# Six cumulative-sum matrices made on the chip by selects instead of loaded, fewer fillers, and a new written order of steps

## The chip, the cores and the metric

The kernel runs on one core of a Trainium2 chip, in one launch. A core has five engines that work from queues of their own: TensorE (PE, matrix products), VectorE (DVE), ScalarE (ACT), GpSimd (POOL), and SyncE (SP), which here mostly starts transfers. They meet through semaphores. Data lies in SBUF (128 partitions); PE writes its products into eight banks of PSUM. The metric is the time of one execution in microseconds on the device: the median of the runs, and lower is better.

## The reference, cut to what matters

Three stages follow one another. An SSM scan over 768 positions for 4 sequences and 8 heads gives 3072 tokens of 256 numbers; an MLP with a squared ReLU follows; then a mixture of experts in which each token goes to one of eight experts.

```python
log_a = np.log(np.clip(a, 1e-06, 1.0))
for c in range(nc):                              # 24 chunks of 32 positions
    cum = np.cumsum(la, axis=-1)                 # within the chunk
    L = np.exp(cum[:, :, :, None] - cum[:, :, None, :]) * causal
    M = np.einsum('bhin,bhjn->bhij', Cc, Bc) * L
    y_intra = np.einsum('bhij,bhjd->bhid', M, xc)
    y_inter = np.einsum('bhin,bhnd->bhid', Cc, state) * np.exp(cum)[:, :, :, None]
    state = decay_full[:, :, None, None] * state + np.sum(Bx, axis=2)
...
h = x @ w_in                                     # (3072, 256) x (256, 2048)
x = (np.maximum(h, 0.0) ** 2) @ w_out            # (3072, 2048) x (2048, 256)
...
logits = xn @ en.T / tau                         # 8 experts
e = np.argmax(logits, axis=1)
out = gate_w * (np.maximum(x @ w1[e], 0.0) @ w2[e])
```

## The kernel before, in words

Tokens are worked in 24 tiles of 128, and the tiles in 6 groups of 4. The scan does a whole tile (128 positions, four chunks of 32) with products on PE: scores of C and B (L821), a multiply by decays on VectorE (L839), a causal select on GpSimd (L847), the product with x (L932), the carried state (L883 and L891, and L899 on GpSimd, which needs `bm_s`, made from c2 in L854) and its product (L927). The decays are exponentials of cumulative sums of log a; PE makes them by multiplying log a with six constant 128x128 matrices, `wm_s[:, 0]` to `wm_s[:, 5]`. Matrices 0 to 3 serve `tables` (L1066), matrix 5 `tables2` (L1080), matrix 4 `tables2` too (L1082) and `ssm_ct0` (L768), which scales C of tiles 0 to 3. Before, the six come with two loads of the constant c1 into the tile `c1_s`: one of 128 x 263 (matrices 4 and 5 and seven columns more), one of 128 x 512 (matrices 0 to 3). A second constant, c2, holds other tables.

In the MLP a unit is 128 of the 2048 hidden columns for one group of 512 tokens, 16 units to a group. Each operand is a pair of 16-bit parts. For a unit, PE does the first product into bank 0 or 1 (L1266), ScalarE the ReLU (L1290), ScalarE or VectorE the square (L1295, L1298), ScalarE the upper part (L1302), VectorE or GpSimd the subtraction that gives the lower part (L1306, L1309), and PE the second product into banks 2 and 3 (L1285). The units of group 0 have code of their own (L1175 and L1214; L1247 and L1250 are their subtractions). `DUE["s2"]` and `DUE["v2"]` are the shares of the units of groups 2 to 5 whose squares are done by ScalarE, and whose subtractions by VectorE. Where a group is done, tokens are routed: logits (L1379), the expert and its weight (L1423 to L1434 on VectorE), places in the expert's list (L1439 to L1445 on PE). For groups 4 and 5 these products lie in bank 7, which shares one tile of PSUM with bank 6, so an instruction on one of the two banks may have to wait for the other. The experts then work in 28 jobs of 128 tokens: first product (L1651, two banks of 0, 1, 4, 5), ReLU and lower part (L1752, L1754), second product (L1692 with L1702, in bank 6 or 2), result (L1719).

All work is written as threads (Python generators) that yield a step at a time with its engine. `weave(th, ORDER)` issues the steps in the order of the list ORDER, one number for each step: it is the thread whose next step is issued. So ORDER alone sets the order of each engine's queue, SP's and GpSimd's among them; what waits for what on the chip follows from the data. A model of the engines' times runs along (`free`, `late`, the numbers that the steps yield); what it decides is how many fillers stand ahead of a step of PE. A filler is a matmul on zeros, 128 x 176, whose result nothing reads (`keep_warm`, L484); 26 stand at the very start. Loads go out on SP (L492), each yielding its step and then `Q.dma_start`. There are eight semaphores for such transfers, used in turn, so the ninth waits for the first to land, and so on. `wide` weights (w_in, w_out) come in four parts each and are converted (L549, L559, L586, L649 to L656) before they are used.

Line numbers here are those of the kernel before. In the changed kernel the same lines stand a little further on: L484 is L485, L492 is L493, L1379 is L1380, and from there to the threads' list five are added, as L1423, now L1428 (L839, L847, L871, L899, L927 and L1066 keep theirs).

## Time and profile before

| | us |
|---|---|
| median of 3 runs (496.10 to 496.74) | 496.70 |
| the profiled execution | 497.33 |
| its span (first to last event of the trace) | 495.6 |
| PE busy | 481.8 (97%) |
| DVE, ACT, POOL busy | 326.9, 345.1, 171.7 |
| DMA moved | 64.52 MB, mean 130 GB/s |

Times in the rows are in us from the span's start unless marked ns. A row of a timeline is one instruction, or several of one kind (x6 is their number), with the time for which the engine had been idle before it and whose end released it. `bank<-wexp` is a product of data in the tile `wexp` into a bank. Matmuls are pipelined: the starts of two that follow one another tell their rate better than their durations. A filler counts as busy. The granted clock is the share of full speed that the throttle granted.

### The profile page before, as it was taken

Reading aid. Unit: us, or ns where it says so; the run is one execution under the profiler, and the core shown is the slowest. Engines: PE = TensorE matmul, PEld = TensorE weight load, DVE = VectorE, ACT = ScalarE, POOL = GpSimd, SP = SyncE. Lnnn points to the kernel's source line nnn. Section 1 sums busy time; section 2 is a strip of 40 time slices with the busy share of each in tenths; the row PEclk is TensorE's granted clock in tenths of the full one; section 3 lists DMA queues with packets and bytes.
Section 4 is the critical chain, followed back from the end, with each engine's and each line's share of the span. In section 5 each row is a group of like instructions: output and inputs, shape, how many; then the busy total and the mean of one; then the engine's idle time right before and its main releaser. Section 6 shows DMA issues by size and latency. Waiting matters only on the chain.

```text
span 495.6 us, 11923 instructions
## 1 busy us (share of the span) xinstructions
PE 481.8 (97%) x4116; PEld 316.1 (64%) x4116; DVE 326.9 (66%) x918; ACT 345.1 (70%) x715; POOL 171.7 (35%) x194
## 2 busy tenths in 40 slices
PE   8999999999999999999999999999899999999994
PEld 8775567677666776767667666766455555555553
DVE  4799988578997889967566865875673343233331
ACT  4799995698879989999999999976332243232321
POOL 2487798544584234600300030030013220220332
PEclk9999999999999999999999999999999999999999
DMA  8970014337155381517224324017887989985980
GB/s 285 400 291 2 2 54 113 102 85 204 16 178 154 44 241 27 151 38 243 72 92 134 113 102 118 13 55 111 140 166 182 196 142 158 188 146 96 158 161 33
DMA packets 112363, 64.52 MB, mean 130 GB/s; under 512 B 101277, under 2 KB 105775, under 8 KB 109232
## 3 DMA queue, kind: packets, MB, share of 16 engines
q1 hardware_dynamic: 105632, 57.22, 47.1%
q0 software_dynamic: 2496, 6.40, 4.4%
q10 hardware_dynamic: 4176, 0.13, 0.8%
q8 instruction: 36, 0.59, 0.5%
q14 instruction: 23, 0.19, 0.1%
HBM read 32.52 MB, written 8.13 MB: 82 GB/s over the span
## 4 chain that ended last, share of the span: by engine, by line
PE 82%; DMA 7%; issue 4%; POOL 3%; DVE 2%; SPq 1%; POOLq 0%; ACT 0%; ACTq 0%; DVEq 0%
PE bank L1266 23%; PE bank L1285 21%; PE bank L1651 12%; PE bank L1692 6%; DMA out<-work 4%; PE bank L1702 3%; PE bank L1214 2%; PE bank L932 2%; PE bank L821 2%; DMA wexp<-in_bc 2%; PE bank L1175 2%; PE bank L927 1%; PE bank L1000 1%; POOL wexp L847 1%; PE bank L1379 1%
## 5 line engine op out<-in xcount | busy, mean ns | idle before, releaser
L1266 PE MATMUL bank<-work 128*128 128x256 f16 x1152 | 135.9, 273 | 1.4 <-POOL work L1250 1.4
L1266 PEld LDWEIGHTS <-work 128*128 128x128 f16 x1152 | 111.9, 98 | 22.8 <-POOL work L1250 1.9
L1285 PE MATMUL bank<-work 128*128 128x512 f16 x480 | 113.3, 379 | 0.0
L1651 PE MATMUL bank<-wexp,work 128*128 x336 | 77.2, 379 | 1.6 <-DVE work L1754 1.6
L1285 PEld LDWEIGHTS <-work 128*128 128x128 f16 x480 | 46.4, 99 | 43.9 <-issue 0.2
L1692 PE MATMUL bank<-wexp,work 128*128 x216 | 71.4, 379 | 0.0
L1754 DVE SCALAR_TENSOR_TENSOR work<-bank,work 128x512 f16<-128x512 f32 x56 | 37.5, 686 | 48.6 <-ACT work L1752 48.6
L1477 POOL DMA_INDIRECT xs<-work x24 | 29.0, 1208 | 105.8 <-ACT work L1302 70.9
L1752 ACT ACTIVATE work<-bank 128x512 f16<-128x512 f32 x56 | 32.2, 597 | 43.6 <-PE bank L1651 36.1
L1726 POOL DMA_INDIRECT out<-work x28 | 27.5, 981 | 97.8 <-DVE work L1719 80.5
L1702 PE MATMUL bank<-wexp,work 128*128 x224 | 60.7, 273 | 0.0
L1306 DVE TENSOR_TENSOR work<-work 128x512 f16<-128x512 f32 x68 | 48.3, 717 | 17.5 <-ACT work L1302 17.3
L1651 PEld LDWEIGHTS <-work 128*128 128x128 f16 x336 | 32.5, 98 | 37.4 <-issue 1.7
L847 POOL TENSOR_SCALAR_AFFINE_SELECT wexp<-wexp 128x512 f32<-128x512 f32 x48 | 37.5, 781 | 53.0 <-DVE wexp L839 30.5
L1290 ACT ACTIVATE work<-bank 128x512 f32<-128x512 f32 x80 | 46.4, 588 | 9.2 <-PE bank L1285 5.6
L1302 ACT CAST work<-work 128x512 f16<-128x512 f32 x80 | 48.4, 613 | 3.4 <-PE bank L1266 2.9
L1709 ACT ACTIVATE work<-bank,work 128x256 f32<-128x256 f32 x28 | 13.2, 474 | 50.4 <-PE bank L1702 43.1
L839 DVE TENSOR_TENSOR wexp<-bank,wexp 128x256 f32<-128x256 f32 x96 | 38.2, 415 | 3.2 <-PE bank L1379 0.8
L1295 ACT ACTIVATE work<-work 128x512 f32<-128x512 f32 x64 | 39.6, 627 | 0.5
L1692 PEld LDWEIGHTS <-work 128*128 128x128 f16 x216 | 21.1, 98 | 25.4
L1719 DVE SCALAR_TENSOR_TENSOR work<-bank,work 128x256 f32<-128x256 f32 x28 | 13.4, 481 | 31.7 <-ACT work L1709 30.0
L1702 PEld LDWEIGHTS <-work 128*128 128x128 f16 x224 | 21.9, 98 | 4.8
(249 smaller groups left out, 755.9 us busy)
## 6 DMA issues: line engine op xcount, KB each, us to landing
wexp<-in_w SPq DMA_DIRECT2D x8, 1024.0 KB, 7.0
work<-in_w SPq DMA_DIRECT2D x8, 1024.0 KB, 4.9
wexp<-in_w_in SPq DMA_DIRECT2D x4, 1024.0 KB, 8.7
wexp<-in_w_out SPq DMA_DIRECT2D x4, 1024.0 KB, 13.7
wexp<-in_x SPq DMA_DIRECT2D x6, 512.0 KB, 6.2
wexp<-in_ct SPq DMA_DIRECT2D x6, 256.0 KB, 7.4
wexp<-in_bc SPq DMA_DIRECT2D x6, 256.0 KB, 5.9
xs<-work SPq DMA_DIRECT2D x9, 132.0 KB, 2.5
```

Of the source, the lines that this page charges most:

```text
L839: V.tensor_tensor(mv, ps.rearrange("p (a b) -> p a b", b=32), eg[:, t, n * q:n * q + n].rearrange("p h q -> p (h q)").unsqueeze(2) .to_bro ...
L847: G.affine_select(out=mm, in_=mm, pattern=[[0, 4], [1, P]], compare_op=ALU.is_ge, fill=0.0, base=0, channel_multiplier=-1)
L1266: T.matmul(po, gg[:, s], wout[:, wi, f], start=(f == 0 and n == 0 and k % 2 == 0), stop=(f == NF - 1 and n == 2), skip_group_check=True)
L1285: T.matmul(p, win[:, wi, kk, f * P:(f + 1) * P], x[:, xi * 2 + kk], start=(n == 0), stop=(n == 5))
L1290: S.activation(r, p, AF.Relu, scale=XK)
L1295: S.activation(r, r, AF.Square)
L1302: S.copy(gh, r)
L1306: V.tensor_tensor(gl, r, gh, ALU.subtract)
L1651: T.matmul(p, xj[i][:, xi * 2 + kk], W[:, bass.ds(e, 1), c0:c0 + 512].rearrange("p a b -> p (a b)"), start=(n == 0), stop=(n == 5))
L1692: T.matmul(po, r[:, f], w2(f, 0, 2 * DM), start=(f == 0), stop=False, skip_group_check=True)
L1702: T.matmul(bank[pbank(j)][:, 0:DM], rT[j % 4][:, 8 + f], W[:, bass.ds(es[j], 1), c0:c0 + 256].rearrange("p a b -> p (a b)"), start=False, ...
L1754: V.scalar_tensor_tensor(out=rh[:, 1, s], in0=p, scalar=0.0, in1=rh[:, 0, s], op0=ALU.max, op1=ALU.subtract)
```

## The change

The two loads of the matrices go, and a new thread `shapes` makes them in `c1_s`: three memsets on VectorE, then nine `affine_select` on GpSimd (a select keeps elements where a linear function of partition and column is at least 0, and writes a constant elsewhere). Only the seven columns behind the matrices (3.5 KB) and the small `rr` are still loaded from c1. `ssm_ct0` waits for matrix 4 and not for c1 and C before its product; it needs C only for its last multiply. The fillers at the start are 22 instead of 26 (21 and one that the model adds), and those behind them 52 instead of 72. `s2` goes from 0.875 to 0.7, `v2` from 1 to 0.92. For groups 4 and 5 the model now knows that routing holds banks 6 and 7 (`mbs`). ORDER is new throughout; of its 2272 numbers before and 2275 now the diff shows a line each.

```diff
-           a2=0.043, ..., s0=1636976993, s1=0.5, s2=0.875, bs=1, qx=84.622, qb=89.036, qc=19.985, q0=89.631,
+           a2=0.043, ..., s0=1636976993, s1=0.5, s2=0.7, bs=1, qx=84.622, qb=89.036, qc=19.985, q0=89.631,
-           pd=95.005, oe=83.994, lj=-6.608, l0=199.952, v0=0.75, v1=0.25, v2=1, ps=176, wq=-6.586, c0=71.046,
+           pd=95.005, oe=83.994, lj=-6.608, l0=199.952, v0=0.75, v1=0.25, v2=0.92, ps=176, wq=-6.586, c0=71.046,
 ORDER = (
-    "0 379 1 5.1 3 5.0 2 9 5.2 10 5.3 4 11 25 12 6.0 16 6.1 379 17 17 7 18 380 47 26 22 23 23 7 7 47 19 7 379 380 "
+    "0 5.0 5.1 1 9 25 5.2 25.0 2 5.3 10 4 11 6.0 12 3 379 3 3 3 17 17 7 380 18 47 21 7 7 379 7 379 26 19 380 47 "
...
     def load_group(g):
...
-        if g == 0:
-            yield "order", ("c1", 0)
         if g:
-            yield "spawn", load(bg[i], bc_tok[:, 4 * g:4 * g + 4, 0], 0.8, ("bc", g), late=1.5 * (g < 2))
+            yield "spawn", load(bg[i], bc_tok[:, 4 * g:4 * g + 4, 0], 0.8, ("bc", g), late=(1.0, 1.5, 0.0)[min(g, 2)])
         else:
-            yield "spawn", load(flat(beo[i][:, 0]), b_t, 0.75, ("bt", g))
+            yield "spawn", load(flat(beo[i][:, 0]), b_t, 0.75, ("bt", g), late=0.8)
...
     def ssm_ct0(k0, k1):
...
-        for key in ("la", "c1", "ct"):
-            yield "need", (key, 0)
+        yield "need", ("la", 0)
...
         V.tensor_copy(lr.rearrange("p (a n) -> p a n", n=N), lf.unsqueeze(2).to_broadcast([P, n * H, N]))
+        yield "need", ("w4", 0)
         yield "T", 0.25 * n, (0,)
...
         S.activation(et, p, AF.Exp)
+        yield "need", ("ct", 0)
         yield "V", 0.07 + 0.135 * n, "L"
...
     def tables2(i):
...
-        yield "need", ("c1", 0)
+        yield "need", ("w4", 0)
+        yield "need", ("w5", 0)
...
-        yield "T", 0.15, (mbk(g),)
+        yield "T", 0.15, mbs(g)
...
+    def mbs(g):
+
+        return (4,) if g < 4 else (6, 7)
...
-        yield "V", VS, (mbk(g),)
+        yield "V", VS, mbs(g)
         V.tensor_tensor(lg, pl, bc8(tq), ALU.mult)
...
+    def shapes():
+
+        w4, w5, w03 = c1_s[:, 4 * P:5 * P], c1_s[:, 5 * P:6 * P], c1_s[:, 0:4 * P]
+        b4 = w4.rearrange("p (a b) -> p a b", b=32)
+        q03 = w03.rearrange("p (q j) -> p q j", j=P)
+        own = c1_s[:, 0:4 * (P + 32)].rearrange("p (q r) -> p q r", r=P + 32)[:, :, 0:32]
+
+        def keep(x, pattern, base, k, fill):
+            G.affine_select(out=x, in_=x, pattern=pattern, compare_op=ALU.is_ge, fill=fill, base=base,
+                            channel_multiplier=k)
+
+        yield "V", 0.5
+        V.memset(w4, -0.5)
+        V.memset(w5, 1.0)
+        V.memset(w03, 1.0)
+        yield "G", 0.75
+        keep(w4, [[-1, P]], -1, 1, 0.5)
+        keep(b4, [[-32, 4], [0, 32]], 0, 1, 0.0)
+        keep(b4, [[32, 4], [0, 32]], 31, -1, 0.0)
+        yield "mark", ("w4", 0)
+        yield "G", 0.25
+        keep(w5, [[-1, P]], -1, 1, 0.0)
+        yield "mark", ("w5", 0)
+        yield "G", 2.3
+        keep(q03, [[32, 4], [0, P]], -1, -1, 0.5)
+        keep(q03, [[32, 4], [0, P]], 31, -1, 0.0)
+        keep(q03, [[0, 4], [-1, P]], -1, 1, 0.0)
+        keep(own, [[-32, 4], [-1, 32]], -1, 1, -0.5)
+        keep(own, [[-32, 4], [0, 32]], 0, 1, 0.0)
+        yield "mark", ("c1", 1)
...
-    k0 = 4 * P, 6 * P + 7
-    th = [(-1e3, log_inputs()), (DUE["lc"], load(c1_s[:, k0[0]:k0[1]], c1[:, k0[0]:k0[1]], 0.5, ("c1", 0))),
-          (DUE["lc"], load(rr_s, c1[0:H, k0[1]:], 0.05, ("c1", 2))), (DUE["lc"], load(c1_s[:, 0:k0[0]], c1[:, 0:k0[0]], 0.75, ("c1", 1), late=1.0)),
-          (DUE["qc"], load(c2_s, c2, 0.75, ("c2", 0), late=1.4)), (2, load_group(0)), (DUE["l1"], load_group(1)), (DUE["ct0"], ssm_ct0(0, 1)), (DUE["ct0"], halves())]
+    k0 = 6 * P + 7
+    th = [(-1e3, log_inputs()), (DUE["lc"], load(c1_s[:, 6 * P:k0], c1[:, 6 * P:k0], 0.1, ("c1", 0))),
+          (DUE["lc"], load(rr_s, c1[0:H, k0:], 0.05, ("c1", 2))), (DUE["lc"], shapes()),
+          (DUE["qc"], load(c2_s, c2, 0.75, ("c2", 0), late=1.0)), (2, load_group(0)), (DUE["l1"], load_group(1)), (DUE["ct0"], ssm_ct0(0, 1)), (DUE["ct0"], halves())]
...
-        keep_warm(26)
-        free.update(T=5.0, S=1.8, V=1.0, G=0.6, Q=0.8)
+        keep_warm(21)
+        free.update(T=4.3, S=1.8, V=1.0, G=0.6, Q=0.8)
         weave(th, ORDER)
```

How the queues stand, at two places. First SP's first transfers; `in_bc` is B by tokens, the load that the state's products need, and `in_b_t` and `in_ct` are B and C as the scores need them. Before:

```order
L492 DMA wexp_71<-in_c1 128x263
L492 DMA wexp_71<-in_ct 128x512
L492 DMA wexp_71<-in_c1 128x512
L492 DMA wexp_71<-in_b_t 128x512
L492 DMA wexp_71<-in_c1 8x128
L492 DMA wexp_71<-in_w_in 128x2048
L492 DMA wexp_71<-in_x 128x1024
L492 DMA wexp_71<-in_w_in 128x2048
L492 DMA wexp_71<-in_bc 128x4x128
L492 DMA wexp_71<-in_c2 128x512
```

and now:

```order
L493 DMA wexp_71<-in_b_t 128x512
L493 DMA wexp_71<-in_ct 128x512
L493 DMA wexp_71<-in_c1 128x7
L493 DMA wexp_71<-in_w_in 128x2048
L493 DMA work_72<-in_emb 8x256
L493 DMA wexp_71<-in_x 128x1024
L493 DMA work_72<-in_tau 128x1
L493 DMA wexp_71<-in_c1 8x128
L493 DMA wexp_71<-in_bc 128x4x128
L493 DMA wexp_71<-in_w_in 128x2048
L493 DMA wexp_71<-in_c2 128x512
```

The two large loads of c1 are gone and b_t is first; B now has one part of w_in ahead of it instead of two; the second stands between B and c2.

The first instructions of GpSimd, before:

```order
L1790 IOTA work 128x18
L1791 IOTA work 128x24
L1805 IOTA work 128x1
L847 AFFINE_SELECT wexp<-wexp 128x512
L751 TENSOR_TENSOR wexp<-wexp 128x512
L847 AFFINE_SELECT wexp<-wexp 128x512 x2
L871 TENSOR_TENSOR wexp<-wexp 128x128
L854 TENSOR_TENSOR wexp<-wexp 128x128
L847 AFFINE_SELECT wexp<-wexp 128x512
L899 TENSOR_TENSOR wexp<-wexp 128x128
```

and now:

```order
L1796 IOTA work 128x24
L1891 AFFINE_SELECT wexp<-wexp 128x128 x4
L1891 AFFINE_SELECT wexp<-wexp 128x512 x3
L1891 AFFINE_SELECT wexp<-wexp 128x4x32 x2
L847 AFFINE_SELECT wexp<-wexp 128x512 x2
L871 TENSOR_TENSOR wexp<-wexp 128x128
L847 AFFINE_SELECT wexp<-wexp 128x512
L750 TENSOR_TENSOR wexp<-wexp 128x512
L847 AFFINE_SELECT wexp<-wexp 128x512
L854 TENSOR_TENSOR wexp<-wexp 128x128
L899 TENSOR_TENSOR wexp<-wexp 128x128
L847 AFFINE_SELECT wexp<-wexp 128x512
```

The nine selects of `shapes` (L1891) stand behind the two IOTAs and ahead of everything that the scan asks of GpSimd; the IOTA of L1805 has gone further back.

The second place is the change from the last routing to the jobs. VectorE before, where bank6 is the tile of banks 6 and 7 and L1754 the lower part of a job's hidden columns, which frees bank 0, 1, 4 or 5:

```order
L1423 TENSOR_TENSOR work_72<-bank6_69,work_72 128x32
L1425 TENSOR_REDUCE work_72<-work_72 128x4
L1427 TENSOR_TENSOR work_72<-work_72 128x32
L1430 SCALAR_TENSOR_TENSOR work_72<-work_72 128x32
L1754 SCALAR_TENSOR_TENSOR work_72<-bank0_63,work_72 128x512
L1432 TENSOR_REDUCE work_72<-work_72 128x4
L1434 TENSOR_TENSOR work_72<-work_72 128x32
L1754 SCALAR_TENSOR_TENSOR work_72<-bank4_67,work_72 128x512
L1754 SCALAR_TENSOR_TENSOR work_72<-bank1_64,work_72 128x512
```

and now:

```order
L1428 TENSOR_TENSOR work_72<-bank6_69,work_72 128x32
L1430 TENSOR_REDUCE work_72<-work_72 128x4
L1432 TENSOR_TENSOR work_72<-work_72 128x32
L1435 SCALAR_TENSOR_TENSOR work_72<-work_72 128x32
L1437 TENSOR_REDUCE work_72<-work_72 128x4
L1439 TENSOR_TENSOR work_72<-work_72 128x32
L1454 TENSOR_TENSOR work_72<-bank6_69,work_72 128x32
L1724 SCALAR_TENSOR_TENSOR work_72<-bank6_69,work_72 128x256
L1759 SCALAR_TENSOR_TENSOR work_72<-bank0_63,work_72 128x512
L1456 TENSOR_TENSOR work_72<-work_72,bank6_69 128x8
L1759 SCALAR_TENSOR_TENSOR work_72<-bank1_64,work_72 128x512
```

L1754 of bank 0 stood behind four instructions of the routing; L1759, the same, now stands behind six of them, L1454 and the result of a job, L1724. PE at the same place, before, from the end of a job's second product:

```order
L1692 MATMUL bank_69<-wexp,work 128x512
L1702 LDWEIGHTS work
L1702 ISA
L1702 MATMUL bank_69<-wexp,work 128x256
L1651 LDWEIGHTS work
L1651 ISA
L1651 MATMUL bank_63<-wexp,work 128x512
```

and now:

```order
L1697 MATMUL bank_69<-wexp,work 128x512
L1707 LDWEIGHTS work
L1707 ISA
L1707 MATMUL bank_69<-wexp,work 128x256
L1380 LDWEIGHTS work
L1380 MATMUL bank_69<-work 128x8
L1380 LDWEIGHTS work
```

Before, the first product into bank 0 (bank_63) follows the second product of the job in bank 6 (bank_69). Now the logits of the last tiles follow it (18 matmuls L1380), then twelve first products into banks 4 and 5, the sums of the routing (L1444 to L1450), 16 matmuls of another second product in bank 2, and then the first product into bank 0.

## Rows read from the trace of the kernel before

**Rows 1.** Page, busy time: engine, us, share of the span, instructions.
```profile
PE 481.8 (97%) x4116; PEld 316.1 (64%) x4116; DVE 326.9 (66%) x918; ACT 345.1 (70%) x715; POOL 171.7 (35%) x194
```
**Rows 2.** Windows: busy us of PE, PEld, DVE, ACT, POOL; granted clock; DMA share; GB/s.
```profile
10.00:15.00 5.00, 5.00 (x101) 4.18 (x100) 3.00 (x8) 3.15 (x5) 2.87 (x4) 1.00 1.04 404
25.00:30.00 5.00, 5.00 (x58) 3.87 (x56) 4.99 (x14) 4.27 (x10) 5.00 (x8) 1.00 1.02 413
60.00:65.00 5.00, 4.80 (x42) 3.82 (x39) 4.90 (x15) 4.69 (x10) 5.00 (x6) 1.00 0.00 0
200.00:250.00 50.00, 50.00 (x421) 34.33 (x419) 34.40 (x98) 48.66 (x105) 11.47 (x11) 1.00 0.44 125
```
**Rows 3.** Timeline of PE, 0 to 36 us: start, us, instruction, [idle before <-releaser].
```profile
1.19 4.00 PE L484 MATMUL bank<-wexp 128*128 128x176 f16 x26 [1.19 <-POOL wexp L1946]
4.98 0.81 PE L1080 MATMUL bank<-wexp 128*128 128x160 f32 x2
...
9.90 0.84 PE L484 MATMUL bank<-wexp 128*128 128x176 f16 x9 [0.34 <-DVE wexp L839]
...
16.81 0.32 PE L883 MATMUL bank<-wexp 128*32 128x64 f32 x8 [0.94 <-POOL wexp L871]
...
18.99 0.49 PE L927 MATMUL bank<-wexp 64*128 64x128 f32 x4 [0.23 <-POOL wexp L899]
...
22.09 1.24 PE L484 MATMUL bank<-wexp 128*128 128x176 f16 x14
23.26 0.73 PE L821 MATMUL bank<-wexp 32*128 32x128 f32 x16
```
**Rows 4.** Line L484: duration ns min/median/max, first and last start.
```profile
L484 PE MATMUL bank<-wexp x98: 236/239/354, 1.2 to 34.0; 128*128 128x176 f16 x98
```
**Rows 5.** The chain that ended last, its longest piece: start us, us, what.
```profile
4.63 11.65 DMA wexp<-in_bc
```
**Rows 6.** Timeline of POOL at 17 us.
```profile
17.03 0.46 POOL L854 TENSOR_TENSOR wexp<-wexp 128x128 f32<-128x128 f32 x1 [0.27 <-DMA wexp<-in_c]
```
**Rows 7.** Timelines of POOL and of DVE, 0 to 9 us.
```profile
1.28 0.14 POOL L1791 IOTA work<- 128x24 int32 x1
8.17 0.13 POOL L1805 IOTA work<- 128x1 int32 x1 [6.75 <-DVE work L1799]
...
6.70 0.49 DVE L788 TENSOR_SCALAR wexp<-wexp,work 128x512 f32<-128x512 f32 x1 [1.88 <-DMA wexp<-in_b_t]
```
**Rows 8.** Line L847, and the timelines around 65 and 87 us.
```profile
L847 POOL TENSOR_SCALAR_AFFINE_SELECT wexp<-wexp x48: 629/635/2665, 10.3 to 210.4; 128x512 f32<-128x512 f32 x48
...
64.79 0.41 PE L1000 MATMUL bank<-wexp 128*128 128x128 f32 x2 [0.20 <-DVE wexp L839]
64.87 2.67 POOL L847 TENSOR_SCALAR_AFFINE_SELECT wexp<-wexp 128x512 f32<-128x512 f32 x1
...
65.77 1.27 DVE L652 SCALAR_TENSOR_TENSOR work<-work 128x1024 f16<-128x1024 f32 x1
...
67.59 0.43 PE L932 MATMUL bank<-wexp 128*32 128x128 f32 x8 [0.85 <-POOL wexp L847]
...
87.35 0.39 PE L1266 MATMUL bank<-work 128*128 128x256 f16 x2 [1.18 <-POOL work L1250]
```
**Rows 9.** Timelines of DVE and PE at 356 to 358 us.
```profile
356.55 0.19 DVE L1423 TENSOR_TENSOR work<-bank,work 128x32 f32<-128x32 f32 x1 [2.29 <-PE bank L1702]
...
357.33 0.69 DVE L1754 SCALAR_TENSOR_TENSOR work<-bank,work 128x512 f16<-128x512 f32 x1
...
358.07 1.46 PE L1651 MATMUL bank<-wexp,work 128*128 x6 [1.56 <-DVE work L1754]
```
**Rows 10.** Groups of instructions by line: busy us, mean ns | idle before.
```profile
L1295 ACT ACTIVATE work<-work 128x512 f32<-128x512 f32 x64 | 39.6, 627 | 0.5
...
L1298 DVE SCALAR_TENSOR_TENSOR work<-bank,work 128x512 f32<-128x512 f32 x16 | 10.9, 683 | 3.4 <-ACT work L1290 3.4
...
L1309 POOL TENSOR_TENSOR work<-work 128x512 f16<-128x512 f32 x12 | 14.4, 1202 | 12.6 <-issue 6.0 <-ACT work L1302 5.8 <-POOL wexp L847 0.8
```

More of the change, by code (lines that the diff above doesn't have):

```diff
@@ L1437, in route @@
         oh4 = flat(ohb)
-        yield "T", 0.62, (mbk(g),)
+        yield "T", 0.62, mbs(g)
         T.matmul(pos, tri_s, oh4, start=True, stop=False, skip_group_check=True)
@@ L1447, in route @@
         S.activation(flat(lg), flat(lg), AF.Exp)
-        yield "V", VS, (mbk(g),)
+        yield "V", VS, mbs(g)
         V.tensor_tensor(tmp32, pos.rearrange("p (t e) -> p t e", e=E), ohb, ALU.mult)
-        yield "V", VS, (mbk(g),)
+        yield "V", VS, mbs(g)
         V.tensor_tensor(base, base, cnt, ALU.add)
@@ L1892, in tile_ssm_mlp_moe @@
             what = raw[:, wi, q], src[:, 2048 * q:2048 * (q + 1)], 2.5, ("raw", wi, q)
-            th.append((DUE["q%d" % q], load(*what, late=1.9)) if wi == 0 else (DUE["r%d" % q], late_load(DUE["g%d" % q], *what, late=1.2)))
+            th.append((DUE["q%d" % q], load(*what, late=1.2)) if wi == 0 else (DUE["r%d" % q], late_load(DUE["g%d" % q], *what, late=1.2)))
     th += [(DUE["la"], logs()), (DUE["pa"], halves_of())]
```

8 lines of the change are left out of this document (4 added, 4 removed), and 173 rows, old and new, of the table ORDER.

## The prediction

> **What bounds the kernel now.** I read the page's busy shares first. TensorE (PE) is busy for 97% of the span [rows 1], so only three things can move the time: less work on PE, shorter waits of PE, and what follows PE's last matmul, which the change leaves alone. The windows came next [rows 2]: in a stage of plain MLP work (200 to 250 us) PE is busy for all 50 us with ScalarE at 48.7, so what the others do there is hidden already; between 60 and 65 us GpSimd is full (5.00 of 5) and PE is not (4.80); from 10 to 30 us the DMA engines are full (share 1.02 to 1.04, 404 and 413 GB/s). The third view was PE's timeline, read for its idle times. At the start PE doesn't look idle, but it is filled up: the fillers (L484) count as busy. 26 of them run from 1.19 to 4.98, 0.146 each, and 14 from 22.09 to 23.26, 0.084 each [rows 3]; with 98 in all [rows 4] they are 26 x 0.146 + 72 x 0.084 = 9.8 us of PE that compute nothing. Between them PE still waits 0.34, 0.94 and 0.23 us, 1.5 in all. Last I looked at who releases those waits. The one at 16.81 ends with B's multiply (L871), which waits for a DMA: the longest piece of the whole chain is the load of B, 4.63 to 16.28 [rows 5]. The one at 18.99 ends with L899, which needs L854, and that waits for c2 (a transfer from in_c) until 17.03 [rows 6].
>
> **The change, part by part.** All terms are against the profiled execution's own time, 497.33 us (span 495.6); the median of the runs shown is 496.7, which is 0.63 less, and I take that off at the end.
>
> *Fillers.* 26 at the start become 22, and 72 later ones 52. That is 4 x 0.146 + 20 x 0.084 = 2.3 us less on PE [rows 3, 4]. A filler that goes is only a gain where PE has something else to do by then; if not, a wait stands in its place. So the term is -2.3, and what waits grow is the next one.
>
> *Loads.* SP's list up to and with the first load of B held 3.81 MB before (128 x 263 and 128 x 512 of c1, ct, b_t, two of w_in, x, bc); now it holds 2.37 MB, since the matrices are no longer loaded and one w_in goes behind. At 404 GB/s [rows 2] B lands 3.6 us earlier, at about 12.7. Next is c2: 4.07 MB before, 3.68 now, so 1.0 us earlier by bytes, about 16.0, and with it the products of tile 1 that L854 and L899 hold back. What stands behind all loads (w_out, the second halves) gains only the 0.39 MB of the matrices, 1.0 us. So PE's work up to tile 1 can come 1 to 3.6 us earlier, and the list takes 2.3 us of fillers out over the same stretch: I take the waits of the start as they are, 0. Bounds: all three waits gone, -1.5; or nothing behind the loads earlier at all, so that each filler becomes a wait, +2.3.
>
> *Selects.* GpSimd makes the matrices between the IOTA at 1.28 and its next instruction at 8.17, before which it is idle for 6.75 us [rows 7]. Nine instructions at the price of the small IOTA (0.14) are 1.3 us; all at the price of the 128x512 select (0.635 [rows 8]) are 5.7. Three are of that size, six are a quarter of it, so I take 3 x 0.64 + 6 x 0.21 = 3.2: behind the IOTA from 1.4 to about 4.6, and at worst to 7.1. (The three memsets that they work on are the first instructions of VectorE, which has its long wait, 1.88 us for b_t, only behind them [rows 7].) The first four, w4 and w5, are done by about 2.3, when PE is still at its fillers (22 x 0.146 = 3.2, to 4.4). PE wants w0 to w3 (L1066) right behind, so it may wait 0.2 us, or 2.7 at worst; that lies ahead of the load of B at 12.7, which ends the wait that counts. I cost it at 0; the 2.7 would show only if B came before the work behind it was done, and the bounds above hold it.
>
> *Decays of C ahead of C's load.* ct0 needs C only for its last multiply. The product and Exp ahead of it no longer wait for a load; this is part of the earlier scores of tile 0, behind which B still has to land. 0 by itself.
>
> *The handover at 358 us.* Before, VectorE's L1423 (the logits of the last group) waits 2.29 us for PE's L1702, because both lie in the tile of banks 6 and 7; three small instructions and then L1754 of bank 0 stand behind it, and PE waits 1.56 us for that [rows 9]. In the new list the second product of that job stands ahead of the logits; PE then has twelve matmuls into banks 4 and 5 (12 x 0.24 = 2.9 by the six in [rows 9]) while VectorE does its six small instructions (0.22 apart, 1.3). Then PE does another job's second product in bank 2, 8 of 512 and 8 of 256 columns, 2.6 us at the rate of the same row; VectorE's queue to bank 0 is L1454, L1724 and L1759, about 0.2 + 0.5 + 0.69 = 1.4. So bank 0 is free 1.2 us before PE wants it. I take -1.4, with a little left for a new wait; bounds -1.56 and +0.5 (if PE waits at L1444 for the small chain).
>
> *The waits in the middle.* PE waits 0.85 us at 67.59 for a select and 1.18 at 87.35 for L1250 [rows 8]; with a smaller one at 64.79 (0.20) that is 2.2. The new list sorts this stretch anew on all engines. Nothing says that it is better or worse: 0, bounds -2.2 and +2.2 (the same again).
>
> *Squares and subtractions.* Of the 64 units of groups 2 to 5, 64 x 0.175 = 11 squares go from ScalarE (0.627) to VectorE (0.683), and 64 x 0.08 = 5 subtractions to GpSimd (1.202) [rows 10]. Where this happens PE is busy for 50.00 of 50 us with ScalarE at 48.66 and VectorE at 34.40 [rows 2]. ScalarE gets some air; VectorE, 11 x 0.68 = 7.5 us over four groups, has room. 0, bounds -0.1 and +1.
>
> Sum: -2.3 + 0 + 0 - 1.4 + 0 + 0 = -3.7; 497.33 - 3.7 - 0.63 = **493.0 us**.
>
> **A rule against the change.** The 128x512 select takes 0.635 at the median and 2.67 once: that one starts at 64.87, VectorE's L652 begins at 65.77 and ends at 67.04, and the select ends 0.5 us after it [rows 8]. The Trainium skill, SBUF — State Buffer, section "SBUF: two separate sides", says why such a thing may be: GpSimd and VectorE's instructions with two SBUF inputs hold one pair of ports as an exclusive lock, and the loser blocks for the whole instruction. The end 0.5 us behind L652 agrees; that the select was first by its start, and lost nevertheless, does not. [...]
>
> **The rivals.**
> A, the forecast: 493.0, with its own range 491.6 to 494.8.
> A+: as A, and the waits in the middle go as well: 493.0 - 2.2 = 490.8. For it: two of them come from single stretched instructions, and a new list seldom hits the same ones. Against: the stretch is as full as before (GpSimd 5.00 of 5 [rows 2]).
> B, the fillers were not the bound: ScalarE and VectorE (4.27 and 4.99 of 5 between 25 and 30 us [rows 2]) or the loads set when the first group is done, and PE waits where it had fillers. With the handover's gain 493.0 + 2.3 = 495.3; without that, which is also the case that the change does little of what it says, 496.7.
> The clock, a later rise: the fillers' spacing falls from 0.146 (176 columns, that is 1.2 GHz) to 0.084 while the granted clock's column stands at 1.00 in all rows; PE did fillers for 3.8 us without a break ahead of it [rows 3]. With 22 fillers and then a wait for the selects the faster level may come later. Price: 4 us of matmuls at half the rate are 2 us, 495.0 if no wait hides them. The Trainium skill, TensorE: Matmul & The Clock Gate, Part 1, has the rule behind it: an idle TensorE is cold and falls to 1.2 GHz. The first row of fillers agrees.
> C, slower: the new list puts more of GpSimd's selects and subtractions beside VectorE's instructions with two inputs. Each hit stretches one by about 2.0 (2.67 for 0.63) and hands about 1.0 of it to PE, as the two of before do (0.85 and 1.18 [rows 8]). Four hits more eat the gain (-3.7 + 4.1 = +0.4); from five on it is slower, 493.0 + 5.1 = 498.1. For it: GpSimd has no slack between 60 and 65 us, and it gets more subtractions at 1.2 each. Against: those come in the later groups, where GpSimd is busy 11.47 of 50 us [rows 2].
>
> **How the numbers follow.** A 0.52, A+ 0.10, B with the handover 0.16, B without 0.07, the clock 0.03, C 0.12. The likeliest is A, so 493.0. What a measurement can tell from no change is about 0.2%, 1.0 us: faster means under 495.7. A, A+ and the clock nearly all, and 0.13 of B's 0.16, lie below it: 0.77. B without the handover, the rest of B and C's mildest make 0.09 for the same. C from five hits on, with a start that is worse than B, 0.14. The range from 490.0 to 497.8 leaves out the better half of A+ and the worse part of C, together under 0.2; its lower end is A+ with a little of the start's -1.5, its upper one the point at which C begins.
>
> **What would show it.** Right: 74 fillers; GpSimd's nine selects done by 4.6 to 6; B landed by about 12.7 and L871 right behind it; tile 1's first product (L927, 18.99 before) at 16 to 17.5; PE's idle before 35 us again 1 to 2 us; no wait of over 0.3 us at the first product into bank 0 behind the last routing; what follows PE's last matmul as long as before. Wrong: waits of 3 us and more before 35 us where the fillers stood (B); fillers at 0.146 beyond the first 22 (the clock); several selects or subtractions of over 2 us with a wait of PE behind each (C).

## The result: slower by 0.65%, and the profile after

The changed kernel takes 501.29 us (median of 13 runs, 498.05 to 503.07), the kernel before 496.83 beside it (13 runs, 496.10 to 501.59). The ratio is 1.0065 with an interval of 1.0038 to 1.0092, that is 1.9 to 4.6 us slower. The forecast was 493.0, and its range ended at 497.8; even the quickest of the 13 runs, 498.05, lies above it. The profiled execution took 499.29, span 497.6.

The page of the changed kernel, its span and the line of TensorE [rows 1]:

```profile
span 497.6 us, 11879 instructions
PE 484.6 (97%) x4092; PEld 317.6 (64%) x4092; DVE 332.8 (67%) x927; ACT 339.5 (68%) x704; POOL 175.2 (35%) x208
```

The share is 97% as before, but with 24 fillers fewer (2.3 us) PE is busy 2.8 us longer. So the same products took some 5 us more of PE. The beginning of PE's timeline answers to [rows 3]:

```profile
1.19 3.41 PE L485 MATMUL bank<-wexp 128*128 128x176 f16 x22 [1.19 <-POOL wexp L1982]
5.31 0.60 PE L1081 MATMUL bank<-wexp 128*128 128x32 f32 x2 [0.72 <-ACT wexp L1043]
9.42 1.24 PE L821 MATMUL bank<-wexp 32*128 32x128 f32 x16
10.87 1.43 PE L1066 MATMUL bank<-wexp 128*128 128x160 f32 x4
13.88 0.73 PE L821 MATMUL bank<-wexp 32*128 32x128 f32 x16
15.12 0.81 PE L1066 MATMUL bank<-wexp 128*128 128x160 f32 x4
19.20 0.49 PE L927 MATMUL bank<-wexp 64*128 64x128 f32 x4
28.06 0.32 PE L883 MATMUL bank<-wexp 128*32 128x64 f32 x8 [0.51 <-DVE wexp L802]
31.21 0.38 PE L987 MATMUL bank<-wexp 128*128 128x1 f32 x2 [0.83 <-DVE wexp L839]
```

The same sixteen products of L821 take 1.24 at 9.42 and 0.73 at 13.88, the same four of L1066 1.43 and 0.81. PE runs at 1.2 GHz to about 12 us, in the kernel before to 5.8. (These are the first entries of the trace's record of the granted clock, 12.31 and 5.76; ahead of them the column of the windows reads 1.00, though the products go at half the rate.) Tile 1's first product (L927) comes at 19.20, no earlier than the 18.99 of before. GpSimd's timeline shows how long the selects take:

```profile
1.38 4.04 POOL L1891 TENSOR_SCALAR_AFFINE_SELECT wexp<-wexp 128x128 f32<-128x128 f32 x9
13.96 0.40 POOL L871 TENSOR_TENSOR wexp<-wexp 128x128 f32<-128x128 f32 x1
18.04 0.46 POOL L854 TENSOR_TENSOR wexp<-wexp 128x128 f32<-128x128 f32 x1
```

All nine are done at 5.42, and B's multiply (L871) follows a select without waiting for its load, 2.4 us before its old place (16.35). What the selects cost PE is told under *Selects* below.

Windows by stage, of the changed kernel and then of another execution of the kernel before (g1 below, 496.33 us); the columns are those of [rows 2]:

```profile
25.00:45.00 20.00, 18.50 (x215) 12.94 (x204) 19.66 (x47) 17.61 (x30) 16.60 (x19) 1.00 0.52 192
45.00:65.00 20.00, 18.80 (x164) 9.29 (x163) 19.41 (x42) 16.89 (x29) 14.84 (x14) 1.00 0.00 1
65.00:90.00 25.00, 24.60 (x300) 20.66 (x300) 21.23 (x46) 19.72 (x39) 20.83 (x24) 1.00 0.17 37
155.00:180.00 25.00, 24.52 (x253) 16.60 (x252) 22.91 (x64) 21.68 (x56) 9.35 (x10) 1.00 0.47 122
345.00:375.00 30.00, 30.00 (x196) 16.23 (x195) 18.42 (x72) 11.55 (x27) 3.41 (x5) 1.00 0.88 144
375.00:405.00 30.00, 29.65 (x162) 15.70 (x161) 13.37 (x42) 8.54 (x17) 7.61 (x9) 1.00 0.94 185
```

```profile
25.00:45.00 20.00, 20.00 (x222) 13.80 (x225) 18.47 (x51) 18.84 (x33) 16.15 (x21) 1.00 0.43 167
45.00:65.00 20.00, 19.70 (x187) 11.63 (x181) 19.82 (x46) 18.40 (x35) 16.68 (x15) 1.00 0.01 2
65.00:90.00 25.00, 22.78 (x265) 17.80 (x264) 18.68 (x37) 16.16 (x34) 23.10 (x24) 1.00 0.45 128
155.00:180.00 25.00, 25.00 (x285) 18.01 (x284) 21.67 (x60) 23.73 (x60) 7.21 (x9) 1.00 0.44 99
345.00:375.00 30.00, 28.44 (x184) 15.21 (x183) 19.79 (x82) 10.59 (x23) 5.07 (x6) 1.00 0.92 162
375.00:405.00 30.00, 30.00 (x166) 16.05 (x164) 10.66 (x28) 8.07 (x16) 6.86 (x7) 1.00 0.85 170
```

The old waits between 65 and 90 us and at the handover are gone but for 0.40 (24.60 for 22.78, 30.00 for 28.44). New ones stand where PE had none: 1.50 us between 25 and 45, 1.20 between 45 and 65 (0.30 before), 0.48 between 155 and 180.

To put a size on each stage I added up, in each trace, PE's products without the fillers, each at its usual spacing, and read how late a kernel is when it has done as much as the profiled execution of before. This **delay** counts fillers, waits and slow products alike. It depends a little on which spacing is called usual: with the mean for it the changed kernel's column at 25 us, where the two lists have done different products, comes out 0.6 lower; the other columns move by 0.2 at most, the last not at all.

| us later than before at | 25 us | 63 | 114 | 155 | 190 | 355 | 372 | end | time |
|---|---|---|---|---|---|---|---|---|---|
| changed kernel | 0.35 | 4.78 | 1.20 | 1.17 | 2.6 | 2.57 | 0.65 | 1.97 | 499.29 |
| e1, the same | -1.56 | 2.88 | -0.70 | -0.73 | 0.7 | 0.64 | -1.28 | 2.09 | 499.40 |
| f1, the same | 2.15 | 6.57 | 3.09 | 2.85 | 4.14 | 4.02 | 2.09 | 3.83 | 501.15 |
| f2, the same | 2.20 | 7.12 | 3.54 | 3.50 | 4.70 | 4.53 | 2.81 | 3.80 | 501.14 |
| f3, the same | 2.28 | 7.19 | 3.61 | 3.48 | 4.87 | 4.46 | 2.64 | 3.84 | 501.16 |
| g1, before | -1.11 | -1.11 | -1.11 | -1.10 | -1.09 | -1.00 | -0.99 | -0.99 | 496.33 |
| g2, before | 2.34 | 2.34 | 2.33 | 2.33 | 2.68 | 2.52 | 2.53 | 2.67 | 500.09 |
| g3, before | -0.22 | -0.21 | -0.21 | -0.20 | -0.20 | -0.25 | -0.24 | -0.11 | 497.32 |

Executions differ at the start, by up to 4 us; from 25 us on these executions of a kernel do nearly the same, but for e1 behind 372 us. Between 25 and 355 us the changed kernel loses 1.87 to 2.33 us, all five times. That isn't the most it can be: e2 and e5 below, which have the same list up to there, lose 3.5 and 4.3, with waits of PE of 0.57 and 0.61 at 163 us and of 0.35 at 166 to 167 that the five don't show.

### The profile page after: what moved, and what is told of

The parts are those of the page before. It is cut to its first block, busy times and chain, and to the rows that moved or that the text cites. A ratio compares the mean times of both kernels' runs of the same rounds, so it can differ in the third digit from the quotient of the medians.

```text
span 497.6 us, 11879 instructions
## 1 busy us (share of the span) xinstructions
PE 484.6 (97%) x4092; PEld 317.6 (64%) x4092; DVE 332.8 (67%) x927; ACT 339.5 (68%) x704; POOL 175.2 (35%) x208
## 4 chain that ended last, share of the span: by engine, by line
PE 53%; issue 14%; DMA 11%; DVE 8%; POOL 4%; SPq 4%; ACT 3%; POOLq 0%; ACTq 0%; DVEq 0%
PE bank L1267 22%; PE bank L1286 17%; DMA out<-work 7%; SPq L1628 3%; PE bank L821 2%; DMA work<-work 2%; PE bank L932 2%; POOL out L1731 2%; PE bank L1656 2%; DMA xs<-work 1%; POOL xs L1482 1%; DVE wexp L839 1%; PE bank L927 1%; DVE work L596 1%; PE bank L1215 1%
## 5 line engine op out<-in xcount | busy, mean ns | idle before, releaser
L1267 PE MATMUL bank<-work 128*128 128x256 f16 x1152 | 138.1, 273 | 0.7 <-DVE work L653 0.5
L1267 PEld LDWEIGHTS <-work 128*128 128x128 f16 x1152 | 111.5, 98 | 23.3 <-issue 1.3
L1286 PEld LDWEIGHTS <-work 128*128 128x128 f16 x480 | 46.2, 99 | 43.1 <-issue 0.3
L1759 DVE SCALAR_TENSOR_TENSOR work<-bank,work 128x512 f16<-128x512 f32 x56 | 37.2, 686 | 44.6 <-ACT work L1757 44.5
L1482 POOL DMA_INDIRECT xs<-work x24 | 26.8, 1118 | 96.0 <-ACT work L1291 32.5
L1656 PEld LDWEIGHTS <-work 128*128 128x128 f16 x336 | 32.6, 98 | 36.8 <-issue 0.4
L1291 ACT ACTIVATE work<-bank 128x512 f32<-128x512 f32 x80 | 46.8, 589 | 12.8 <-PE bank L1286 4.4
L1307 DVE TENSOR_TENSOR work<-work 128x512 f16<-128x512 f32 x63 | 43.3, 692 | 17.3 <-ACT work L1303 17.2
L847 POOL TENSOR_SCALAR_AFFINE_SELECT wexp<-wexp 128x512 f32<-128x512 f32 x48 | 35.0, 729 | 53.2 <-DVE wexp L839 35.9
L1714 ACT ACTIVATE work<-bank,work 128x256 f32<-128x256 f32 x28 | 13.1, 474 | 45.8 <-PE bank L1707 42.6
L839 DVE TENSOR_TENSOR wexp<-bank,wexp 128x256 f32<-128x256 f32 x96 | 38.2, 414 | 7.6 <-ACT work L1123 2.7
L1697 PEld LDWEIGHTS <-work 128*128 128x128 f16 x216 | 21.1, 98 | 25.2
L1724 DVE SCALAR_TENSOR_TENSOR work<-bank,work 128x256 f32<-128x256 f32 x28 | 13.3, 479 | 35.3 <-ACT work L1714 33.6
L1310 POOL TENSOR_TENSOR work<-work 128x512 f16<-128x512 f32 x17 | 20.4, 1203 | 41.7 <-ACT work L1303 36.3
L1296 ACT ACTIVATE work<-work 128x512 f32<-128x512 f32 x53 | 33.1, 625 | 0.6
```

Source lines behind the costliest of these rows:

```text
L839: V.tensor_tensor(mv, ps.rearrange("p (a b) -> p a b", b=32), eg[:, t, n * q:n * q + n].rearrange("p h q -> p (h q)").unsqueeze(2) .to_bro ...
L847: G.affine_select(out=mm, in_=mm, pattern=[[0, 4], [1, P]], compare_op=ALU.is_ge, fill=0.0, base=0, channel_multiplier=-1)
L1267: T.matmul(po, gg[:, s], wout[:, wi, f], start=(f == 0 and n == 0 and k % 2 == 0), stop=(f == NF - 1 and n == 2), skip_group_check=True)
L1286: T.matmul(p, win[:, wi, kk, f * P:(f + 1) * P], x[:, xi * 2 + kk], start=(n == 0), stop=(n == 5))
L1291: S.activation(r, p, AF.Relu, scale=XK)
L1307: V.tensor_tensor(gl, r, gh, ALU.subtract)
```

## The experiments

"Model's time" below is that of the scheduler's model that sets the fillers. In kernels made of both lists and kept in the code of before, line numbers are 8 higher than before.

**e1: the changed kernel again.** No edit.

> The changed kernel once more, for a second profile and more times. The theory (the clock): TensorE runs at the lower of its two rates until about 12.3 us, where before it rose at 5.8, because it waits 0.72 us behind its 22 first fillers and then has only small products; how late the rise comes differs from run to run. It expects 498 to 502 us again, and in this profile the products at 5 to 10 us (scores of tile 0, 16 products of L821) in about 1.2 us again and not in 0.73, unless the run is one of the quickest. The rival (VectorE as the bound between 22 and 34 us, with instructions stretched beside GpSimd's) expects the same time but does not need slow products at the start; a spread of several us between runs is not explained by it.

Measured: 501.28 (6 runs), ratio 1.0082 [1.0061, 1.0104]. The traced execution is the quickest of the six. Its start is early (L821's sixteen take 0.73 at 7.55), so it is 1.9 us ahead of the first trace at 25 us, though PE then waits 0.99 us at 10.91, in L1107, which multiplies by `rr`, for the load of 8x128 from c1 (4 KB). It loses the lead at one place: PE waits 2.20 us for an expert job's result, of which ScalarE's L1714 is the first step.

```profile
10.91 0.36 PE L1107 MATMUL bank<-wexp 8*128 8x20 f32 x2 [0.99 <-DMA wexp<-in_c]
378.46 0.38 PE L1697 MATMUL bank<-wexp,work 128*128 x1 [2.20 <-DVE work L1724]
```

```profile
377.05 0.47 ACT L1714 ACTIVATE work<-bank,work 128x256 f32<-128x256 f32 x1 [8.34 <-PE bank L1656]
```

The product that L1714 reads had ended at 372.4; in the first trace the same instruction started at its product's end (374.35). Why it started 4.7 us late, the trace doesn't show.

**e2, e4: more fillers at the start** (27 and 51 in all, for 22), **e3: fewer in the kernel before.**

```diff
-        keep_warm(21)
+        keep_warm(26)    # e2; 50 in e4
```

```diff
-        keep_warm(26)
+        keep_warm(22)    # e3, the kernel before
```

> The changed kernel with 27 fillers at the start instead of 22, nothing else. The five cost 5 x 0.146 = 0.73 us of TensorE, in which it now waits 0.72 for ScalarE's L1043: nothing by itself. Clock theory: without the break the faster rate comes at about 6 us, the products from 5.3 to 12.3 take about half, tile 0 is done 2 to 3 us earlier, and the time falls by 2 to 3 us to 496 to 498, with less spread. Rival (VectorE's chain): no change, 499 to 502.

> The changed kernel with 51 fillers at the start instead of 22, nothing else: 29 more, at 0.146 until the rate rises and 0.08 behind that, so that the first products wait until about 7.8 us instead of 5.3. Clock theory: the fillers raise the rate whatever the data do, the products behind them run at the faster rate and end no later than now (7.8 + 7/2 = 11.3 against 12.3), so it is 1 us or more faster than the changed kernel, about 497 to 499, with little spread. Rival: 2.5 us of work more at the start, so 499 to 504, slower than the changed kernel or the same.

> The kernel before with 22 fillers at the start instead of 26, nothing else. Clock theory, in the form that a break in TensorE's work is what delays the rise: its next products (L1080) have their data by about 4.4 us, so there is no break, the rate rises at about 6 as before, and the time is the same or 0.6 us less (4 fillers): 496 to 497. In the form that the number of fillers counts, the rise comes later and it is 1 to 3 us slower than before: 498 to 500. The rival (VectorE's chain) expects 496 to 497.

Measured: e2 500.79 (9 runs), 1.0066 [1.0039, 1.0092]; e4 500.70 (6), 1.0049 [1.0030, 1.0068]; e3 496.95 (12), 0.9999 [0.9976, 1.0022]. In the trace e2 was at full rate at 5.2 and fell back from 12.0 to 15.4 us; e4 reached it at 7.1. Neither kernel is as fast as the clock theory had it (496 to 498, 497 to 499); both lie where the rival had them. Both traces have the early rise, but so has e1, with 22 fillers and on the same chip, so they don't show that fillers bring it. And the early rise is worth hardly any time here: in e2 it met the load of `rr` (PE waits 1.9 us for it) and lost the rest in the fall, both lose in the middle (3.5 and 2.2 us from 25 to 355 us), and both have the late L1714 (PE waits 2.3 in e2). In the kernel before, 22 fillers cost and gain nothing.

**e5 to e8: each part of the list by itself.** e5 is the changed kernel with the old list from the jobs on (355 us); e6 the kernel before with the new list from there; e7 the changed kernel up to tile 2 (its first 128 numbers, about 24 us), then the old list and shares; e8 the kernel before with the new list and shares between that place and the jobs. Besides ORDER, e8 holds the fillers behind 24.5 us of the model's time to four for a step, since the model doesn't know the mixed list:

```diff
-                keep_warm((s - free[eng]) * (DUE["warm"] if s > 8.3 else DUE["cold"]))
+                keep_warm(min((s - free[eng]) * (DUE["warm"] if s > 8.3 else DUE["cold"]), 99 if s < 24.5 else 4))
```

> The changed kernel with its new list up to the first step of an expert job (its first 1770 numbers), and from there what is left in the order of the old list. Theory: the new list of the jobs is what costs most: in the second profile of the changed kernel the gain of the handover (1.9 us) is there, but at 376 us TensorE waits 2.2 us for L1724, the result of a job, because ScalarE's L1714 starts 4.7 us after the product it reads. So this kernel has the old wait of 1.6 us at the handover, and no wait over 1 us behind it; against the changed kernel it gains about 1 us (2.9 - 1.9) where the wait came and loses 1.9 where it did not: 499 to 500.5 us. Rival (the loss lies ahead of the jobs and the jobs' list is all gain): 1.5 to 2 us slower than the changed kernel, 501.5 to 503.

> The kernel before with its old list up to the first step of an expert job (1758 numbers), and from there what is left in the order of the new list; nothing else is changed. Theory: the handover's wait of 1.6 is gone, and a wait of about 2.2 us at a later result and two of 0.3 to 0.5 come in most runs: 1 us slower than before, 498 to 499.5 where before is 497 to 498. Rival (the loss lies ahead of the jobs): 1.5 to 2 us faster than before, 495 to 496.5.

> The changed kernel (selects, 22 first fillers, loads in their new order) with the new list up to the products of tile 2 (its first 128 numbers, to about 24 us), and from there what is left in the order of the old list, with the old shares of squares and subtractions. 74 fillers as in the changed kernel. Theory (the new order of the conversions is what costs between 24 and 65 us, where the second profile loses 4.4 us though the start was 1.6 us ahead): that loss goes, the waits of before in the middle (2.2 us) and at the handover (1.6) come back, and the time is that of before less the 1 to 1.6 us that the start brings where the clock rises early, 495.5 to 497.5. Rival (ScalarE's and VectorE's work, or w_out's landing, sets when the first group is done, in whatever order): the start's gain is lost again by 40 us and it is 497.5 to 499.

> The kernel before (loaded matrices, 26 first fillers) with the old list up to the products of tile 2 (120 numbers), then the new list's order up to the first job, with its shares of squares and subtractions, then the old order of the jobs. From tile 2 on at most 4 fillers stand ahead of a step, some 18 in all. Theory (the new order of the conversions costs about 4.4 us between 24 and 65 us and gives 3.5 back up to 115, and 1.4 are lost up to 180): 2 us slower than before, 499 to 500.5. Rival (the cause is the new start and not the order behind it): no slower than before, 495 to 497.5.

| | median us (runs) | ratio | delay in the middle (25 to 355 us) | from 355 us to the end |
|---|---|---|---|---|
| e5 | 502.15 (12) | 1.0071 [1.0042, 1.0101] | 4.3 | 0.4 |
| e6 | 496.74 (12) | 0.9995 [0.9973, 1.0016] | -0.2 (0 to 345 us) | 0.3: -1.9 by 372, +1.5 by 387, +0.7 behind |
| e7 | 499.11 (12) | 1.0027 [1.0005, 1.0050] | -0.2 | 0.4 |
| e8 | 501.52 (6) | 1.0074 [1.0049, 1.0098] | 4.9 | 0 |

So the loss in the middle goes with the new middle list (e5, e8) and is absent where the old one stands (e6, e7). The new start by itself costs something (e7). The handover's gain is real, and the new list of the jobs gives it back (e6, by its trace; the times don't tell it from nothing). Two things make e8's 4.9 larger than the list alone: 17 more fillers stand behind 25 us than before (23 for 6, up to 1.4 us), and its trace is the slowest of its six executions. Against what was expected, e5 came out as its rival had it, e6 between its two, e7 just above its rival's range, since its rate rose late (at 13.7 us), and e8 1.0 us above its theory.

**e9 to e12: the middle cut in two, the squares, the handover alone.** e9 has the new list from tile 2 to group 2, e10 from group 2 to the jobs; both are the kernel before otherwise, with e8's bound on fillers; e10 has the new shares. e11 is e10 with 62 of the 64 squares on ScalarE:

```diff
-        if int(sq * (u + 1)) > int(sq * u):
+        if int(sq * (u + 1)) > int(sq * u) or g > 1 and u % 8 < 7:
```

e12 is the kernel before with one number of its list moved, so that VectorE frees bank 0 ahead of the logits:

```diff
-    295 295 295 295 329.0 295 333
+    329.0 295 295 295 295 295 333
```

> The kernel before with its own list up to tile 2, the new list from there to the first unit of group 2, and then its own list again; the shares of squares and subtractions as before; behind 24.5 us of the model's time no step gets more than four fillers. Theory 1 (the new order loses at two places, each by itself): TensorE is 4.4 to 5.4 us late by 63 us, has most of it back by 115 us, and stays 1.0 to 1.6 us late to the end: ratio to the kernel before 1.002 to 1.0035. Theory 2 (the loss that lasts comes only from group 2 on, with the changed shares): 0 by 150 us, ratio 0.999 to 1.001. Theory 3 (the first place sets off the second): 2.5 to 4 us late from 176 us on, ratio 1.005 to 1.008.

> The kernel before with its own list up to the first unit of group 2, the new list from there to the jobs, with the new shares (0.7 of the squares on ScalarE, 0.92 of the subtractions on VectorE), and its own list for the jobs. Theory 1 (two places, each by itself): level to 155 us, 1.3 to 2.8 us late by 180 us and to the end: ratio 1.0025 to 1.0055. Theory 3 (the second place only follows from the first): within 0.5 us all the way, ratio 0.999 to 1.001.

> As the one before it, but 62 of the 64 squares of groups 2 to 5 on ScalarE (before: 56; with the new share: 45), in the same list. If the squares on VectorE are what costs at 155 to 180 us: the delay there goes, ratio 0.999 to 1.001. If the order of the steps is: as the one before it, ratio 1.0025 to 1.0055, or up to 1 us more where ScalarE becomes the one that TensorE waits for.

> The kernel before with one number of its list moved: the lower part of bank 0 of one expert job (L1754) stands on VectorE ahead of the four routing instructions that begin with L1423, and not behind them. Both theories: the wait of 1.56 us at 358 us goes. If the gain stays: 1.2 to 1.6 us less at the end, ratio 0.997. If the next jobs wait for something else that does not come earlier (what follows from the routing, which is not moved): the gain is given back by 405 us, ratio 0.999 to 1.001.

Measured: e9 503.88 (6 runs), 1.0120 [1.0091, 1.0149]; e10 499.26 (12), 1.0021 [0.9995, 1.0048]; e11 502.31 (6), 1.0094 [1.0066, 1.0121]; e12 496.99 (12), 0.9992 [0.9969, 1.0014]. e9 lies above all three of its theories, and e10's interval touches both of its own. Cutting a list makes waits of its own where the pieces meet, here of e9 and of e10:

```profile
148.13 0.33 PE L807 MATMUL bank<-wexp 128*128 128x128 f32 x1 [2.51 <-DVE wexp L810]
```

```profile
152.26 0.38 PE L714 MATMUL bank<-work 128*128 128x1 f32 x2 [1.26 <-ACT wexp L709]
```

Behind its wait e9's PE also falls back to the lower rate for 3.4 us. That is most of what e9 and e10 lose there (4.3 and 1.9 us), so these two don't say how the 2.2 us divide. e11 answers its question: with the squares on ScalarE the delay at 155 to 180 us is no smaller (2.4 us), and 2.2 more come by 340 us (PE 158.70 of 160 us busy between 185 and 345, ScalarE 150.0; in e10 159.96 and 145.0). The new share of squares doesn't cause the loss; in this list, which was made with it, it helps.

In e12 the wait of 1.56 us, which both theories had gone, becomes one of 0.44:

```profile
358.04 2.75 PE L1659 MATMUL bank<-wexp,work 128*128 x12 [0.44 <-DVE work L1762]
```

PE is 0.87 us earlier behind it, and that stays to the end but for 0.17. The timing can't tell 0.17% from nothing. What follows from the routing is not what holds the next jobs up; in e6 and the changed kernel it is their own new order.

**f1 to f3 and g1 to g3: three more executions of each, with traces.**

> The changed kernel as it is. If the start's rate and the late result at 376 us come with the change: fillers at 0.146 us or products at half rate beyond 9 us in most of its executions and in none of the kernel before, and a wait of over 1 us at L1697 about 376 us in about half. If chance brings them to both kernels: as often in the kernel before. The middle (25 to 355 us) again 2 to 3 us longer than before.

> The kernel before as it is. If the start's rate comes with the change: full rate by 6 us (5.8 in its first trace) and no fall behind it, and no wait but those of its first trace over 0.3 us. If it is chance: a start at half rate to 12 us or a fall in one of three executions, which costs 2 to 5 us.

(f2, f3, g2 and g3 repeat these.) Measured: 501.15, 501.14, 501.16 and 496.33, 500.09, 497.32 us, in the table above. None of the three of the changed kernel shows the late L1714, which was expected in about half. Windows of f1, with PE's granted clock as the third column from the end:

```profile
16.00:20.00 4.00, 4.00 (x87) 2.96 (x84) 3.72 (x12) 3.59 (x9) 2.88 (x5) 0.96 1.06 406
20.00:23.00 3.00, 3.00 (x33) 2.55 (x31) 1.51 (x4) 2.48 (x6) 1.33 (x2) 0.50 1.01 411
23.00:26.00 3.00, 3.00 (x49) 2.25 (x47) 2.16 (x8) 1.58 (x3) 1.47 (x4) 0.99 1.01 414
```

Its rate rose at 12.8 us, fell back at 19.7 (the column shows 0.50) and rose again at 23.1, all while PE was busy without a break. By the trace's record of the granted clock, over all traces:

| start | traces | full rate first at | falls back later |
|---|---|---|---|
| old list (before, g1 to g3, e3, e6, e8 to e12) | 11 | 4.0 to 6.6 us, all | 4 of 11, for 3.4 to 6.8 us |
| new list, 22 fillers (changed, e1, f1 to f3, e5, e7) | 7 | 12.3 to 17.2 us in 6; 5.0 in e1 | 2 of 7, for 3.4 us |
| new list, 27 or 51 fillers (e2, e4) | 2 | 5.2 and 7.1 us | e2, for 3.4 us |

On three chips both starts were traced (f1, f2, g1 and g2; f3 and g3; e5 to e8): there the old start rose early in five traces of five, and the new one, with 22 fillers, late in five of five. So the late rise belongs to the new start. How far its 22 fillers are what counts isn't shown: e1 to e4 ran on a fourth chip, where the new start rose early with 22, 27 and 51. The fall behind it comes to both kernels.

## Why the prediction was wrong

Two terms of its sum failed, a third ended too early, and one rival got far too small a chance.

**Fillers and start: -2.3 predicted.** Against the kernel before in the same table (mean of its four executions at 25 us: +0.25) the changed kernel's start is -1.8 in e1 and +0.1 to +2.0 in the others. Where the rate rises early the gain is near the forecast; in six of seven traces with this start it doesn't. The step that failed is the term *Fillers*, -2.3, taken as if PE came to full rate where it did before (5.8 us); the runs showed 12.3 to 17.2 us. The prediction names this as the rival "The clock", gives it 2 us, which e1 against the changed kernel confirms (1.9 at 25 us), and then a chance of 0.03. What in the new start delays the rise is open. Fewer fillers alone don't: e3, the kernel before with 22, rose at 4.1. A gap behind them alone doesn't either. Ahead of the early rise, in the kernel before, PE did fillers without a break to 4.98 and products behind them without idle time, and in the changed kernel it is idle 0.72 us from 4.6; but e1 had the same idle time (0.73) and an early rise, f3 was idle for only 0.19 there and rose last of all (17.2), and f1 fell back without idle time. The Trainium skill, TensorE: Matmul & The Clock Gate, Part 1, has it that an idle TensorE is at the lower clock; the first fillers of all 20 traces, 0.147 us apart, agree, and no more follows from it here. Nor is an early rise worth all of its 1.9: e1 and e2 then wait 0.99 and 1.9 us for `rr`. *Loads* summed the bytes as far as B and c2 and left out this one of 4 KB. It is eighth in SP's list where it was fifth, behind x and a part of w_in; in the kernel before, its product (L1106) stands at 8.30 without a wait. That is rival B, the loads, behind the clock.

*Loads* came earlier as predicted: B is there by 13.96 at the latest, where its multiply stands without a wait (in e1 the multiply waits for it until 11.66; 12.7 was forecast). But PE's waits at 16.81 and 18.99 [rows 3], 0.94 and 0.23, were that execution's: g1, g2 and g3 have neither, and g1 is 1.11 us earlier from there on. Most of the -1.5 that I gave as their bound was not there to be had.

**The waits in the middle: 0 predicted, +1.87 to +2.33 measured**, at the upper end of the bounds (2.2). This is the second step that failed: a zero because nothing said that the new list is better or worse. The old waits went, as case A+ had it, and the new list brought others of more weight: 0.51 and 0.83 at 28.06 and 31.21, then 0.65, 0.27, 0.20 and 0.47 to 65.4 us, 0.17 and 0.18 between 166 and 176, all but the 0.20 for VectorE, which is busy 39.07 of 40 us from 25 to 65. It was nearly as full before (38.29 in g1), with PE busy for 39.70 of the 40, so a full VectorE alone doesn't make these waits; what differs is the order in which the work stands. The prediction read VectorE's room where the MLP runs alone (200 to 250 us). Its rival B had VectorE's 4.99 of 5 between 25 and 30 us, but only as a price of the fillers; this term didn't use it. Part of VectorE's time there is stretching, the mechanism of rival C. VectorE's and then GpSimd's timeline around the first two waits, and then both in g1:

```profile
24.73 1.53 DVE L979 TENSOR_TENSOR work<-work 128x256 f16<-128x256 f32 x1
27.50 0.41 DVE L802 TENSOR_TENSOR wexp<-bank,work 128x256 f32<-128x256 f32 x1
28.43 1.40 DVE L979 TENSOR_TENSOR work<-work 128x256 f16<-128x256 f32 x1
```

```profile
24.14 1.83 POOL L593 TENSOR_TENSOR wexp<-wexp 128x512 f32<-128x512 f32 x1
28.26 1.30 POOL L593 TENSOR_TENSOR wexp<-wexp 128x512 f32<-128x512 f32 x1
```

```profile
21.99 0.42 DVE L979 TENSOR_TENSOR work<-work 128x256 f16<-128x256 f32 x1
24.13 1.20 DVE L979 TENSOR_TENSOR work<-work 128x256 f16<-128x256 f32 x1
23.75 1.30 POOL L592 TENSOR_TENSOR wexp<-wexp 128x512 f32<-128x512 f32 x1
```

L979 takes 0.42 where it starts first (21.99 in g1, GpSimd's next at 22.16) and 1.20 where it comes into GpSimd's L592 (24.13 in g1); now both of its instances are hit, 1.53 and 1.40, and each ends 0.3 us behind GpSimd's instruction. That is 1.3 us more of VectorE than in g1. L802 and L839, for which PE waits at 28.06 and 31.21, are queued behind them; that the hits make the waits is read from this order, not tested. The Trainium skill, SBUF — State Buffer, section "SBUF: two separate sides", says that the loser of the shared ports blocks for the whole instruction, and here the rows agree. So C, at 0.12, was partly what happened; not five hits, but one more than before, with a full VectorE behind it.

The idle times explain part of the 2.2: from 25 to 345 us PE is idle 3.6 us in the changed kernel and 2.65 in g1, 0.9 more; seven more fillers stand behind 25 us (13 for 6), 0.6. The rest I put down to restarts, since behind a wait the spacing grows by more than the idle time (0.33 for 0.17 at 166.39, 0.45 for 0.18 at 176.03); that is worked out, not tested. How the loss divides over places stays open, since e9 and e10 have seams.

**Squares and subtractions: 0.** The squares are not what costs, as far as e11 tests it (with 62 of them on ScalarE it is worse); the subtractions weren't tested by themselves.

**The handover: -1.4 predicted, -1.72 to -1.93 measured** in the five traces from 355 to 372 us. Right, but the sum ended there. The new order of the jobs behind it has no term at all and takes 1.0 to 1.7 us back by the end, 3.4 in e1 with the late L1714. The net is -0.19 to -0.73, and +1.45 in e1; e6 shows it apart.

**Selects: 3.2 predicted, 4.04 measured**, done at 5.42 within the 4.6 to 6 given; the six small ones take 0.28 to 0.32 each, not 0.21. Their cost to PE was put at 0, by what PE reads of them alone. They cost about 0.4 by another way: VectorE's L1041, the first step of log a, starts at 4.11 beside a select and takes 0.67 instead of 0.26, and ScalarE's L1043 and PE's first product, at 5.31, follow it. In f3 L1041 takes 0.26, and that product stands at 4.78, having waited only 0.19, there for the selects. The 74 fillers and the stretch behind PE's last matmul (7.0 us in both) were right.

By these terms a typical changed execution, f1, is 2.15 + 1.87 - 1.93 + 1.74 = 3.83 us behind the profiled execution of before. The nine traces together differ by 2.7 us in their means (500.43 and 497.77), inside the interval of the ratio.

## What to carry to other kernels

When a written order is replaced as a whole, a zero for "sorted anew" is the boldest term of the sum: every stage of a new one needs a term, above all where two engines are over 90% busy (here PE and VectorE at 25 to 65 us). When a start is made anew, ask when PE will come to full rate, and give a late rise a real chance: here it came in six traces of seven, for a chance of 0.03. Follow every load that the first products read; here one of 4 KB held PE for 0.99 to 1.9 us as soon as the rate was no longer what held it. And ask what a new job for an idle engine does to its neighbour's instructions, as the selects do to L1041. One profiled execution can hold a wait of chance (B at 16.81); more traces of the kernel before, taken first, would have shown which waits come every time.
